# The first three pieces of the float64 weights asked for by ScalarE's queue instead of SP's

## The chip, the cores and the metric

The kernel runs on one core of one Trainium2 chip. The metric is the device time of one execution in microseconds (us); less is better. A core has five engines with a queue each: TensorE (PE in the profile; its weight loads are PEld), VectorE (DVE), ScalarE (ACT), GpSimd (POOL) and SyncE (SP), and 16 DMA engines that all queues feed.

## The reference

An attention block, a mixture of three linear layers joined by a maximum, and a mixture of experts, all on 2304 tokens of 512 numbers:

```
attn  = softmax(mask(scale * q @ k.T)) @ v          # 4 batches, 8 heads, 576 tokens, 64 wide, mask by blocks of 64
x     = attn laid out as (2304, 512)
h     = maximum(maximum(x @ w1, x @ w2), x @ w3)    # w1, w2, w3: (512, 768), given as float64
x     = h @ w_out                                   # (768, 512), float64
score = x @ w_skip;  e = argmax(x @ w_gate)         # 8 experts
out   = x + gate * (max(x @ m2_w1[e], 0) @ m2_w2[e])  where score > 0, else x
```

## The kernel before

The 2304 tokens are taken in six chunks of 384 (three tiles of 128). For each chunk the attention of four pairs of heads is computed in units: one unit is one tile of queries (128 or 64) of one pair of heads in one chunk. A unit goes over PE (scores, `sc`, L611 and a mask matmul L618), DVE (row maximum, L631, scaled at L645), ACT (exponential into `p`, L656), DVE and ACT (reciprocal L671, scaling of `p`, L677 and L679), PE (transposes `tp`, L691), ACT or DVE (copy to `pT`, L696), PE (product with V, `pv`, L710), and ACT and DVE (the result as a high and a low part in `x`, L720 and L718). Scores have two buffers in PSUM (`sc`), so the third unit's scores wait until the first unit's exponentials have read theirs.

The weights w1, w2 and w3 come as float64. Each is cut into six pieces of 128 columns, 18 pieces in all, numbered k = 3f + i for column block f and matrix i. A piece is 512 KB of raw words. It is loaded into `raw` (three buffers, L494), then decoded: ACT takes the absolute value of the upper words (`ab`, L503, into `dec`, two buffers), DVE runs four integer steps (`dec`, L511, L513, L515, L517), ACT rounds to a high part (`hi`, L528), DVE subtracts for the low part (`lo`, L532). A `dec` buffer is free again after `lo`, so the absolute value of piece 2 waits for `lo` of piece 0. Six pieces of w_out follow in the same way. The hidden layer of a chunk (`ps_h`, L736) takes 12 matmuls a piece and can start when all attention of the chunk is in `x`.

The order of all this up to the last chunk is set by a planner: `build` (from L157 on) makes a task of each step with an engine, a duration, a due time, what it depends on and which buffers it takes, and `Plan.order` lays them out engine by engine, taking among the tasks that can start the one with the smallest due time. For a DMA it adds the bytes over one common line of 230 GB/s and 2 us. The tasks are then written out in the order of their planned starts, and each engine runs its own in that order: an instruction that waits holds back all that stand behind it on the same engine. SP's queue holds the loads: K and Q of a group (four transfers of 96 KB, L579 and L580), V (L587), the identity for the transposes (L958) and the raw pieces.

In the kernel before, piece 0 stands in SP's queue behind the loads of the first three groups, pieces 1 and 2 behind those of the fourth.

Of the kernel before, what the change touches and what calls it, by code (L numbers as in the profile page):

```python
# [17 lines left out]
B, H, S, D = 4, 8, 576, 64  # L18
# [138 lines left out]
def build(S, E, groups, units):  # L157
# [4 lines left out]
    def later(name, t, *readers):  # L162
        for r in readers:
            r.releases.append((name, t))
# [18 lines left out]
    for i, (c, b, qlo, qhi, tiles, hp) in enumerate(groups):  # L183
        at = when[first_of[i]] - 12
# [19 lines left out]
    for ks in su:  # L204
        at = when[ks[0]]
        dur, acq, deps = 0.0, [], [start]
        for k in ks:
            i, c, hp, q0, nq, nk, col, first = units[k]
# [5 lines left out]
        for n, k in enumerate(ks):  # L214
            i, c, hp, q0, nq, nk, col, first = units[k]
            at = when[k]
# [37 lines left out]
        for k in ks:  # L254
            i, c, hp, q0, nq, nk, col, first = units[k]
# [10 lines left out]
        for k in ks:  # L266
            i, c, hp, q0, nq, nk, col, first = units[k]
# [19 lines left out]
    later("hm", c1, c2)  # L287
    for k in range(18 + NF):
        at = first_w + w_pace * k if k < 18 else 16 + 3.0 * (k - 18)
        raw = S.add("SP", 0.6, at - 8, lambda k=k: E.raw(k), [], ["raw"], nbytes=524288)  # L290
        ab = S.add("ACT", 0.55, at, lambda k=k: E.ab(k), [raw], ["dec"])
        d = ab
        for n, dur in enumerate((0.335, 0.335, 0.6, 0.6)):
            d = S.add("DVE", dur, at, lambda k=k, n=n: E.dec(k, n), [d])
        later("raw", raw, d)
        hi = S.add("ACT", 0.51, at - 1, lambda k=k: E.hi(k), [d])
        lo = S.add("DVE", 0.6, at - 1, lambda k=k: E.lo(k), [hi])
        later("dec", ab, lo)
        piece[k] = [hi, lo]
        if k >= 18:  # L300
            tw = S.add("PE", 0.45, at, lambda k=k: E.tw(k), [d, c1], ["mo"])
            later("dec", ab, tw)
            wt = S.add("ACT", 0.46, at - 4, lambda k=k: E.wt(k), [tw], ["y"])
            later("mo", tw, wt)
            pw = S.add("PE", 0.9, at, lambda k=k: E.pw(k), [wt], ["mo"])
            wp = S.add("DVE", 0.16, at - 4, lambda k=k: E.wp(k), [pw])
            later("mo", pw, wp)
            later("y", wt, pw)
            piece[k].append(wp)

    prev_y, prev_l, rk_prev = [], [], None
    for c in range(NCH):
# [3 lines left out]
        for f in range(NF):  # L316
            for i in range(3):
                at = base + (3 * f + i) * 2.1
# [22 lines left out]
        at = base + 38  # L341
# [39 lines left out]
    for q in range(8):  # L381
        deps = [go] if q < 3 else [free] if q == 3 else split[q - 4]
        raw = S.add("SP", 0.6, base - 20 + 4 * q, lambda q=q: E.expert_raw(q), deps, nbytes=1 << 20)
        if q < 6:
# [4 lines left out]
            for i in range(2):  # L389
                at = base + 4 * q + 2 * i  # L390
# [54 lines left out]
def _moe1_phase(tc, nc, const, small, g):  # L445
# [12 lines left out]
    with ExitStack() as st_y:  # L458
# [29 lines left out]
        raw_at, dec_at, wt_at, ps_at = {}, {}, {}, {}  # L488

        def raw_words(k):  # L490
            raw = raw_at[k] = apool.tile([P, 4 * P, 2], I32, tag="raw", name="raw", bufs=3)
            if k < 18:
                f, i = divmod(k, 3)
                nc.sync.dma_start(  # L494
                    out=raw.rearrange("p (c f) t -> p c (f t)", c=ND),
                    in_=ws[i][:, 2 * f * P:2 * (f + 1) * P].rearrange("(c p) f -> p c f", p=P))
            else:
                f = k - 18
                nc.sync.dma_start(out=raw.rearrange("p f t -> p (f t)"), in_=w_out[f * P:(f + 1) * P, :])
# [57 lines left out]

        E.wc = wp_copy
        E.raw, E.ab, E.dec, E.hi, E.lo = raw_words, absolute, decode, hi_part, lo_part
        E.tw, E.wt, E.pw, E.wp = wo_turn, wo_turned, wo_route, wo_routed  # L560

# [457 lines left out]

        work = Plan(dict(sc=2, tp=2, mo=2, p=3, pT=2, raw=3, dec=2, hm=4, y=2, k=6, q=3, v=2, x=2))  # L1020
        build(work, E, groups, units)
        with tc.manual_schedule():
            for t in work.order():
# [576 lines left out]
```

## Time and profile before

| | |
|---|---|
| three runs, median (lowest to highest) | 609.37 us (606.86 to 609.39) |
| the profiled execution, its own time | 609.76 us |
| its span, first to last instruction | 607.1 us |
| busy in the span: PE, DVE, ACT | 582.6, 349.8, 316.7 us |
| mean granted TensorE clock | 0.994 |
| first exponential of the attention on ACT | 7.08 us |
| first matmul of the hidden layer (`ps_h`) | 41.33 us |
| first absolute value of a raw piece on ACT | 17.99 us |

The profiled execution lies 0.4 us above the median of the three runs, and its span 2.7 us under its own time. A granted clock of 1.00 is the upper of TensorE's two levels, 2.4 GHz; 0.994 is the mean over the span.

The timeline gives for each instruction its start and length, and in brackets how long its engine had been idle and what ended that. The view by stages gives what each engine was busy in a stretch, so stretch less busy is idle time. SP's row in a timeline is the time that its queue took to issue a transfer; how long that then took to land stands in the list of DMA issues.

### The profile page before, as it was taken

How to read it: one execution, taken by the hardware profiler on the slowest of the kernel's cores; microseconds unless marked ns; L12 is line 12 of the kernel's file. 1: busy time of each engine (PE TensorE's matmuls, PEld its weight loads, DVE VectorE, ACT ScalarE, POOL GpSimd, SP SyncE). 2: the span in 40 equal slices, each digit the busy share in tenths (PEclk: the TensorE clock that was granted, in tenths of full speed). 3: DMA queues.
4: the chain of work that ended last, by engine and by line, in shares of the span. 5: the costliest groups of instructions: out<-in, count | busy, mean ns of one | idle time of the engine just before them, and what ended most of it. 6: DMA issues, size and time to landing. Idle time of an engine off the chain costs nothing. (4 is left out here: it accounts for less than half of the span.)

```text
span 607.1 us, 11847 instructions
## 1 busy us (share of the span) xinstructions
PE 582.6 (96%) x4338; PEld 495.5 (82%) x4338; DVE 349.8 (58%) x1022; ACT 316.7 (52%) x825; POOL 43.3 (7%) x101
## 2 busy tenths in 40 slices
PE   6889999899999999999999999999999999899994
PEld 3568798699888998988978889988899997688732
DVE  4899999925555346555366562565533675258600
ACT  4998869942757424545245444375641541158420
POOL 1000000002000010000200000200001011311101
PEclk9999999999999999999999999999999999899998
DMA  6564754421110220103211223100016752799980
GB/s 184 159 203 140 217 159 142 138 92 60 51 30 23 72 90 24 41 21 94 75 44 48 62 77 110 44 22 23 1 37 213 250 179 49 238 363 366 343 288 23
DMA packets 61096, 72.74 MB, mean 120 GB/s; under 512 B 7571, under 2 KB 40597, under 8 KB 61024
## 3 DMA queue, kind: packets, MB, share of 16 engines
q1 hardware_dynamic: 59424, 68.88, 35.5%
q0 software_dynamic: 1600, 2.96, 1.5%
q8 instruction: 39, 0.64, 0.5%
q14 instruction: 33, 0.27, 0.1%
HBM read 61.13 MB, written 11.04 MB: 119 GB/s over the span
## 5 line engine op out<-in xcount | busy, mean ns | idle before, releaser
L736 PE MATMUL ps_h<-x,w 128*128 128x384 f32 x1296 | 244.7, 341 | 0.5 <-DVE hm L745 0.5
L736 PEld LDWEIGHTS ps_h<-x,w 128*128 128x128 f32 x1296 | 222.4, 188 | 5.5 <-issue 3.3
L656 ACT ACTIVATE p<-sc,nm 128x288 f32<-128x288 f32 (+7 forms) x168 | 85.0, 516 | 29.6 <-DVE nm L645 28.9
L696 ACT COPY pT<-tp 128x512 f32<-128x512 f32 (+2 forms) x108 | 53.3, 511 | 47.9 <-PE tp L691 46.7
L611 PE MATMUL sc<-k,q 64*64 64x288 f32 (+9 forms) x384 | 67.8, 453 | 6.4 <-DMA q<-in_kq_dram 4.7
L691 PE MATMUL tp<-cst_sb,p 128*128 128x128 f32 x432 | 65.9, 281 | 3.9 <-ACT pT L696 1.8
L787 PE MATMUL ps_y<-wo,h_h 128*128 128x256 f32 (+1 forms) x360 | 68.8, 287 | 0.0
L691 PEld LDWEIGHTS tp<-cst_sb,p 128*128 128x128 f32 x432 | 49.7, 143 | 17.7 <-issue 8.0
L710 PE MATMUL pv<-pT,vt 128*64 128x128 f32 (+1 forms) x960 | 60.4, 270 | 1.6 <-ACT pT L696 1.5
L631 DVE TENSOR_REDUCE nm<-sc 128x2 f32<-128x256 f32 (+7 forms) x64 | 51.3, 811 | 15.8 <-PE sc L618 10.3
L710 PEld LDWEIGHTS pv<-pT,vt 128*64 128x64 f32 x960 | 48.0, 138 | 13.8 <-issue 4.9
L787 PEld LDWEIGHTS ps_y<-wo,h_h 128*128 128x128 f32 x360 | 56.7, 189 | 1.2 <-issue 1.2
L787 PE MATMUL ps_y<-wo,h_l 128*128 128x256 f32 (+1 forms) x180 | 51.1, 284 | 0.0
L611 PEld LDWEIGHTS sc<-k,q 64*128 64x128 f32 (+1 forms) x384 | 29.5, 178 | 24.2 <-issue 11.3
L677 ACT ACTIVATE p<-p,r 128x576 f32<-128x576 f32 (+8 forms) x73 | 42.3, 596 | 9.0 <-DVE r L671 8.3
L745 DVE TENSOR_TENSOR hm<-ps_h,ha 128x384 f32<-128x384 f32 x36 | 20.0, 555 | 34.6 <-PE ps_h L736 33.2
L720 ACT CAST x<-pv 128x128 fp32r<-128x128 f32 (+1 forms) x80 | 20.0, 263 | 31.2 <-PE pv L710 30.8
L656 ACT ACTIVATION_READ_ACCUMULATOR p<-sc,nm 128x1 f32 x168 | 35.0, 208 | 0.0
L745 DVE TENSOR_TENSOR hm<-ps_h,hm 128x384 f32<-128x384 f32 x36 | 20.0, 555 | 25.2 <-PE ps_h L736 24.6
L787 PEld LDWEIGHTS ps_y<-wo,h_l 128*128 128x128 f32 x180 | 34.0, 189 | 0.0
L718 DVE TENSOR_TENSOR x<-pv,x 128x128 fp32r<-128x128 f32 (+1 forms) x80 | 21.1, 274 | 21.6 <-ACT x L720 20.8
L749 ACT CAST h_h<-hm 128x384 fp32r<-128x384 f32 x36 | 18.5, 515 | 28.0 <-DVE hm L745 27.9
(220 smaller groups left out, 678.8 us busy)
## 6 DMA issues: line engine op xcount, KB each, us to landing
raw<-in_m_w_dram SPq DMA_DIRECT2D x19, 1024.0 KB, 7.2
raw<-in_w_dram SPq DMA_DIRECT2D x18, 512.0 KB, 3.8
vt<-in_v_dram SPq DMA_DIRECT2D x16, 320.0 KB, 3.3
x<-y SPq DMA_DIRECT2D x18, 256.0 KB, 2.1
out_dram<-y SPq DMA_DIRECT2D x18, 256.0 KB, 2.4
xa<-in_m_w_dram SPq DMA_DIRECT2D x4, 1024.0 KB, 6.8
xb<-in_m_w_dram SPq DMA_DIRECT2D x4, 1024.0 KB, 7.8
raw<-in_w_out_dram SPq DMA_DIRECT2D x6, 512.0 KB, 3.5
```

What stands on the lines that cost most here:

```text
L611: nc.tensor.matmul(bank[:, 0:hi - lo], gd["q"][rows, q0:q0 + nq], gd["k"][rows, lo:hi], start=True, stop=packed or hi != nk)
L631: nc.vector.tensor_reduce(nm, first_ps[:, :, 0:w], axis=AX.X, op=ALU.max, negate=True)
L656: nc.scalar.activation(u["p"][:, j, lo:hi], src, AF.Exp, bias=u["nm"][:, j:j + 1], scale=0.125, accum_out=u["su"][:, n, j:j + 1])
L677: nc.scalar.activation(pt, pt, AF.Copy, scale=r)
L691: nc.tensor.transpose(tp[:, n, :], u["p"][:, j, t * P:(t + 1) * P], ident)
L696: copy(u["pT"][:, m:m + z], u["tp", m][:, 0:z])
L710: nc.tensor.matmul(pv[64 * j:64 * j + 64, 0:nq], vt[:, t, 64 * j:64 * j + 64], pT, start=(t == 0), stop=(t == nkt - 1))
L718: nc.vector.tensor_tensor(xl, pv, xh, op=ALU.subtract)
L720: nc.scalar.copy(xh, pv)
L736: nc.tensor.matmul(ps, a[:, d, :], x[:, d, :], start=(n == 0), stop=(n == 3 * ND - 1))
L745: nc.vector.tensor_tensor(nxt, hm_at["ps", i], hm_at[f], op=ALU.max)
L787: nc.tensor.matmul(ps, a[:, f, hs], x[:, f, lo:hi], start=(n == 0), stop=(n == 3 * NF - 1))
```

## The change

In the planner's `build`, the load of pieces 0, 1 and 2 becomes a task of ACT with the due times -900, -899 and -898 (ahead of all other work but the masks), and it is entered with 150,000 bytes rather than 524,288. In `raw_words` the transfer of these three is issued from ACT's queue. The other 15 pieces and w_out stay with SP. The bytes that move are the same.

```
+        first = k < 3
-        raw = S.add("SP", 0.6, at - 8, lambda k=k: E.raw(k), [], ["raw"], nbytes=524288)
+        raw = S.add("ACT" if first else "SP", 0.6, k - 900 if first else at - 8, lambda k=k: E.raw(k), [], ["raw"],
+                    nbytes=150000 if first else 524288)
...
         def raw_words(k):
+            dma = nc.scalar.dma_start if k < 3 else nc.sync.dma_start
             raw = raw_at[k] = apool.tile([P, 4 * P, 2], I32, tag="raw", name="raw", bufs=3)
             if k < 18:
                 f, i = divmod(k, 3)
-                nc.sync.dma_start(
+                dma(
```

Since the planner lays everything out anew, the order of other work changes too, in the attention of the first chunks. Line numbers of the kernel after are up to 3 higher. On ACT, from the start of the program, before (`warm` is a first exponential that loads the table; `p`, `sc` and `nm` belong to attention units):

```order
L955 ACT_TABLE_LOAD
L955 ACTIVATE warm_135<-warm_135 128x2
L656 ACTIVATE p_186,su_187<-sc_165,nm_181 128x128 x2
L656 ACTIVATE p_191,su_192<-sc_170,nm_184 128x256
L677 ACTIVATE p_186<-p_186,r_199 128x128
```

and on ACT in the same place now:

```order
L497 DMA raw_129<-in_w1_dram 128x4x256
L958 ACT_TABLE_LOAD
L958 ACTIVATE warm_137<-warm_137 128x2
L497 DMA raw_156<-in_w2_dram 128x4x256
L497 DMA raw_158<-in_w3_dram 128x4x256
L506 ACTIVATE dec_163<-raw_129 128x512
L531 CAST w0_113<-dec_163 128x512
L506 ACTIVATE dec_196<-raw_156 128x512
L506 ACTIVATE dec_202<-raw_158 128x512
L659 ACTIVATE p_205,su_206<-sc_177,nm_194 128x128 x2
```

The three issues, the three absolute values and one high part now stand ahead of the first exponential. On DVE, behind the same seven memsets, before:

```order
L631 TENSOR_REDUCE nm_181<-sc_165 128x2
L645 TENSOR_SCALAR nm_181<-nm_181 128x2
L631 TENSOR_REDUCE nm_184<-sc_170 128x2
L645 TENSOR_SCALAR nm_184<-nm_184 128x2
L667 TENSOR_SCALAR r_199<-su_187 128x2
L671 RECIPROCAL r_199<-r_199 128x2
```

and on DVE in the same place now:

```order
L514 TENSOR_SCALAR dec_163<-dec_163 128x512
L516 TENSOR_SCALAR dec_163<-dec_163 128x512
L518 SCALAR_TENSOR_TENSOR dec_163<-raw_129,dec_163 128x512
L520 SCALAR_TENSOR_TENSOR dec_163<-raw_129,dec_163 128x512
L634 TENSOR_REDUCE nm_194<-sc_177 128x2
L535 TENSOR_TENSOR w0_113<-dec_163,w0_113 128x512
L648 TENSOR_SCALAR nm_194<-nm_194 128x2
L634 TENSOR_REDUCE nm_200<-sc_183 128x2
L514 TENSOR_SCALAR dec_196<-dec_196 128x512
L648 TENSOR_SCALAR nm_200<-nm_200 128x2
L516 TENSOR_SCALAR dec_196<-dec_196 128x512
L514 TENSOR_SCALAR dec_202<-dec_202 128x512
```

The decoding of piece 0 (`dec_163`) moved ahead of the first maximum, and steps of pieces 1 and 2 (`dec_196`, `dec_202`) stand among the first units. Up to the first maximum over a hidden layer (L745), DVE had run 29 steps of decoding in the order before and runs 40 in the one after, of them 4 ahead of the first maximum of the attention. On ACT, up to the first copy out of a hidden layer (L741), 11 steps of decoding stood before and 15 stand after, of them 4 ahead of the first exponential.

## Rows read from the trace of the kernel before

**Rows 1.** Busy time by stages: stretch, its length, each engine's busy us (instructions), clock, DMA.

```profile
core 0: us, PE busy (x) PEld busy (x) DVE busy (x) ACT busy (x) POOL busy (x), PEclk, DMA share, GB/s
0.00:20.00 20.00, 13.94 (x88) 8.73 (x88) 10.72 (x45) 11.15 (x37) 1.87 (x13) 1.00 0.71 203
20.00:40.00 20.00, 15.99 (x145) 9.62 (x143) 19.43 (x62) 19.78 (x63) 0.15 (x1) 1.00 0.50 146
...
41.30:122.00 80.70, 78.39 (x643) 66.76 (x640) 77.70 (x212) 67.09 (x174) 2.54 (x13) 1.00 0.55 166
...
120.00:500.00 380.00, 379.37 (x3007) 344.20 (x3006) 195.71 (x601) 182.32 (x502) 22.78 (x53) 1.00 0.22 71
```

**Rows 2.** Timeline of PE: first scores, and first matmuls of the hidden layer.

```profile
4.00 0.76 PE L611 MATMUL sc<-k,q 64*128 64x128 f32 x2 [4.00 <-DMA q<-in_kq_dram]
...
41.33 4.45 PE L736 MATMUL ps_h<-x,w 128*128 128x384 f32 x24
```

**Rows 3.** Timeline of ACT: the table load and the first exponential.

```profile
0.75 1.28 ACT L955 ACT_TABLE_LOAD   x1 [0.75 <-PEq L1587]
...
7.08 0.37 ACT L656 ACTIVATE p<-sc,nm 128x128 f32<-128x128 f32 x1 [4.83 <-DVE nm L645]
```

**Rows 4.** Timeline of DVE: the first maximum and its scaling.

```profile
6.35 0.42 DVE L631 TENSOR_REDUCE nm<-sc 128x2 f32<-128x256 f32 x1 [4.78 <-PE sc L618]
6.81 0.17 DVE L645 TENSOR_SCALAR nm<-nm 128x2 f32<-128x2 f32 x1
```

**Rows 5.** Timeline of SP's queue: first load, and the raw pieces.

```profile
0.74 0.59 SPq L579 DMA_DIRECT2D k<-in_kq_dram  x1
...
9.93 0.59 SPq L494 DMA_DIRECT2D raw<-in_w_dram  x1
...
13.04 1.14 SPq L494 DMA_DIRECT2D raw<-in_w_dram  x2
```

**Rows 6.** DMA issue at 0.74 us: KB, us from issue to landing.

```profile
k<-in_kq_dram SPq DMA_DIRECT2D x1, 96.0 KB, 2.3
```

**Rows 7.** The same for the two issues at 9.93 and 10.56 us.

```profile
raw<-in_w_dram SPq DMA_DIRECT2D x1, 512.0 KB, 4.5
k<-in_kq_dram SPq DMA_DIRECT2D x1, 96.0 KB, 4.3
```

**Rows 8.** Busy time by stages, the first 18 us.

```profile
0.00:4.00 4.00, 0.00 (x1) 0.03 (x1) 0.58 (x7) 1.49 (x2) 1.87 (x13) 1.00 0.37 109
4.00:6.00 2.00, 1.27 (x6) 1.01 (x8) 0.00 (x0) 0.00 (x0) 0.00 (x0) 1.00 0.61 167
6.00:8.00 2.00, 1.43 (x11) 0.77 (x7) 1.19 (x3) 0.81 (x4) 0.00 (x0) 1.00 0.70 195
...
2.00:10.00 8.00, 4.70 (x20) 2.70 (x20) 2.29 (x8) 2.35 (x11) 0.55 (x1) 1.00 0.69 196
...
12.00:14.00 2.00, 2.00 (x10) 1.26 (x10) 1.46 (x7) 1.88 (x7) 0.00 (x0) 1.00 1.02 303
15.00:18.00 3.00, 3.00 (x24) 1.86 (x20) 1.80 (x8) 2.34 (x9) 0.00 (x0) 1.00 1.02 331
```

**Rows 9.** Instructions on the decoded words: duration min/median/max in ns, first and last start.

```profile
L503 ACT ACTIVATE dec<-raw x10: 663/690/708, 18.0 to 56.2; 128x512 f32<-128x512 f32 x10
L511 DVE TENSOR_SCALAR dec<-dec x10: 405/420/427, 18.9 to 58.3; 128x512 f32<-128x512 f32 x10
L513 DVE TENSOR_SCALAR dec<-dec x10: 416/420/428, 19.7 to 58.8; 128x512 int32<-128x512 int32 x10
L515 DVE SCALAR_TENSOR_TENSOR dec<-raw,dec x10: 681/688/693, 20.1 to 59.2; 128x512 int32<-128x512 int32 x10
L517 DVE SCALAR_TENSOR_TENSOR dec<-raw,dec x9: 679/683/691, 21.0 to 57.7; 128x512 int32<-128x512 int32 x9
L528 ACT CAST w<-dec x9: 607/627/659, 22.2 to 58.7; 128x512 fp32r<-128x512 f32 x9
L532 DVE TENSOR_TENSOR w<-dec,w x9: 676/683/692, 24.3 to 59.8; 128x512 fp32r<-128x512 f32 x9
```

## The prediction

> **What bounds the kernel now.** I read the busy times by stages first. From 120 to 500 us PE is busy 379.37 of 380 us [rows 1]: whatever the first 120 us end late or early, the end inherits, since nothing behind can swallow it. So the question is how much time PE loses early. It loses 6.06 us in the first 20 and 4.01 in the next 20 [rows 1], of which 4.00 before its first scores [rows 2] and 0.73 and 0.57 up to 8 us [rows 8]; that leaves 4.77 us between 8 and 40. From 41.3 to 122 us it loses 80.70 - 78.39 = 2.31 us [rows 1]. These 7.1 us are all that a better order could win once the scores have begun.
>
> Then the timelines. The first maximum runs at 6.35, its scaling at 6.81, the first exponential at 7.08 [rows 3, 4]. Up to there ACT and DVE stand idle 4.83 and 4.78 us in one wait: the idle time that is to be filled. From 20 to 40 us both are full (19.78 and 19.43 of 20), and DVE stays so up to 122 us (77.70 of 80.70) [rows 1]. The hidden layer starts at 41.33 [rows 2].
>
> **The change part by part.** *What goes from SP.* Three issues of about 0.59 us [rows 5] leave its queue and later K and Q are asked for sooner. PE's idle time names a DMA only for the first two scores, whose loads stood ahead of the pieces anyway: worth nothing.
>
> *What ACT gets as its first work.* One issue ahead of the table load, two behind it, each 0.59 us by SP's row [rows 5]. Table load and issues end at about 0.75 + 1.28 + 3 x 0.59 = 3.8 us, under the wait that lasts to 7.08 [rows 3]: nothing. Without that cover it would cost 1.8 us.
>
> *What now stands ahead of the first exponential.* In the order after, ACT runs the absolute values of pieces 0, 1 and 2 and the high part of piece 0 before it. The third absolute value needs piece 2 landed, and the buffer that the low part of piece 0 on DVE frees. Behind it wait every exponential; on DVE, a step of piece 2 that stands ahead of the first sums and reciprocals; on PE, the transposes and the third unit's scores, which need a buffer that exponentials free. So the attention starts at the later of two times, plus 0.69 us for that absolute value [rows 9].
>
> First time, the chain over piece 0. A 96 KB load lands 2.3 us after its issue [rows 6]; at 303 GB/s, the rate with several transfers in flight [rows 8], 0.32 us of that is moving, so 2.0 us are fixed. Piece 0 moves 0.524 MB; alone at 331 GB/s [rows 8] that is 1.6 us, landing at 0.75 + 2.0 + 1.6 = 4.35. Absolute value, four steps, high part, low part, third absolute value: 0.69 + 0.42 + 0.42 + 0.69 + 0.68 + 0.63 + 0.68 + 0.69 = 4.90 [rows 9], and eight handovers of 0.07 (from 6.35 to 7.08 pass 0.73 us for 0.42 + 0.17 of work, two handovers [rows 3, 4]) make 0.56: first exponential not before 9.8.
>
> Second time, the landing of piece 2. Three pieces are 1.573 MB. Meanwhile SP goes on asking for K, Q and V: from 2 to 10 us the DMA engines moved 196 GB/s [rows 8] with no piece among it. With several queued they move 303 to 331 [rows 8], 317 in the middle. Which of two queues goes first, no row shows. If the pieces get everything, 1.573 / 0.331 = 4.75 us, landing at 7.5, and the chain above decides: 9.8. If SP is served first, 317 - 196 = 121 are left, 13.0 us, landing at 15.75, exponential at 16.4. With equal shares, 158 each, 9.9 us, landing at 12.65, exponential at 13.3. I take equal shares: with both on SP's queue, K asked for right behind a piece took 4.3 us against 2.3 before and the piece 4.5 [rows 6, 7], so both suffer. Delay against 7.08: **6.3 us**, bounds 2.7 and 9.4.
>
> The Trainium skill's page "DMA: Bandwidth & Descriptors" (section "Queues, rings and completion order") says that each DMA engine goes round robin over the queues that have work, a packet at a time; by that rule the time would be that of equal shares, and no run here shows two hardware queues at once. Its section "Issuing engines are not separate DMA queues" speaks against the change: another issuing engine saves only its issue time.
>
> *What K and Q lose.* Under equal shares their loads move at 158 rather than 196 GB/s, so the first scores at 4.00 come perhaps 1 us later. That is hidden under the 13.3; if the pieces come quickly it is part of the 9.8.
>
> *What is given back.* The decoding done early should lighten the full stretch. By counts of the order it does not do so before the hidden layer starts: ACT has 11 steps of decoding between the first exponential and the first copy out of the hidden layer, before and after (15 less 4); DVE has 29 before and 36 after (40 less 4). The planner has filled the room with later pieces. Seven more steps of some 0.6 us [rows 9], 4 us, go into the idle time of DVE between its first maximum and 18 us. So the hidden layer starts about as much later as the attention, and what is given back comes behind it, where more pieces lie ready: at most the 2.31 us that PE loses there. I take half, **1.1 us**, with bounds 0 and 2.3.
>
> **Sum.** 6.3 - 1.1 = 5.2 us more than the profiled execution's 609.76: 615.0. That execution lies 0.4 above the median of the three runs, 609.37, so for a median: **614.6 us**.
>
> **The rivals.** *Fast landing.* If the pieces take nearly all of the transfers, or SP's loads leave more room than I think, the chain over piece 0 decides: 2.7 us less 0 to 2.3, so 609.8 to 612.1. For it: the DMA share is only 0.61 to 0.70 from 4 to 8 us [rows 8]. Against it: 1.57 MB more in the same time.
>
> *SP first.* If K, Q and V keep their pace, piece 2 lands at 15.75: 9.4 less 0 to 1.1, so 617.7 to 618.8. For it: SP has one short transfer outstanding after the other; against it: nothing known prefers them.
>
> *Faster.* This is what the idle 4.8 us of DVE invite. With the fast landing (+2.7), three pieces would be decoded while the units start: 3 x (0.42 + 0.42 + 0.69 + 0.68 + 0.68) = 8.7 us of DVE's work [rows 9] leave the full stretch, and PE's 4.77 and 2.31 us of losses [rows 1, 8] could all go: 609.4 + 2.7 - 7.1 = 605.0. It decides from where PE's losses between 8 and 40 us shrink by more than the first exponential is late. Against it: the counts, which show no lighter stretch, and that the first exponential must wait for the last of the three pieces.
>
> *The change does not do what it says:* the transfers start at once, but the planner enters 150,000 bytes for 524,288, so its order expects piece 2 sooner than any of the landings above. That is the cause in the forecast, not another case.
>
> **How the numbers follow.** Forecast (equal shares, give or take 2 us) 0.60; fast landing 0.20; SP first 0.11; faster 0.09. A measurement can tell about 0.5%, 3.05 us, from no change: slower means above 612.4, faster below 606.3. The forecast lies above 612.4 but for its edge, SP first wholly, the fast landing within: slower 0.70, same 0.22, faster 0.08. The range goes from the foot of the fast landing, 609.8, to SP first with nothing given back, 618.8; outside lie the faster case and some 0.05 above.
>
> **What would show it.** In the trace after: the first exponential at 13.3 us (9.8 to 16.4), right behind the third absolute value, ACT's idle time before that ended by the raw piece's DMA and not by DVE; the three pieces landing at about 6, 9 and 12.7 us; PE idle some 5 us between the second unit's scores and the first transposes; the hidden layer from about 47 us; PE full behind 120 us as before. Wrong it would be if the third absolute value ran by 10 us, if the hidden layer started before 43 us, or if PE's losses from 41 to 122 us, 2.31 us, were not there to give and more were lost there by the new order.

## The result and the profile after

The changed kernel takes 613.23 us (median; 612.18 to 614.43) against 609.18 for the kernel before on the same chip: 1.0061 times as long, 95% interval 1.0045 to 1.0076. In a second comparison (E6 below) it took 614.72 against 610.36: 1.0083, 1.0061 to 1.0104. By these ratios it is slower by 3.7 and 5.1 us, by the medians by 4.05 and 4.36; the forecast was 5.2 us, 614.6. The execution profiled for the rows below took 613.26 us with a span of 611.2 (before: 609.76 and 607.1).

The timeline of ACT after, from the start (start, length, engine, line, what; in brackets the idle time before it and what ended it):

```profile
0.75 0.43 ACTq L497 DMA_DIRECT2D raw<-in_w_dram  x1
1.21 1.28 ACT L958 ACT_TABLE_LOAD   x1 [1.21 <-PEq L1590]
1.61 1.18 ACTq L497 DMA_DIRECT2D raw<-in_w_dram  x2
...
4.50 0.66 ACT L506 ACTIVATE dec<-raw 128x512 f32<-128x512 f32 x1 [1.79 <-DMA raw<-in_w_dram]
7.56 0.62 ACT L531 CAST w<-dec 128x512 fp32r<-128x512 f32 x1 [2.41 <-DVE dec L520]
9.50 0.66 ACT L506 ACTIVATE dec<-raw 128x512 f32<-128x512 f32 x1 [1.32 <-DMA raw<-in_w_dram]
12.48 0.66 ACT L506 ACTIVATE dec<-raw 128x512 f32<-128x512 f32 x1 [2.32 <-DMA raw<-in_w_dram]
13.05 0.35 ACT L659 ACTIVATE p<-sc,nm 128x128 f32<-128x128 f32 x1
```

The first exponential runs at 13.05, 5.97 us later than in [rows 3], right behind the third absolute value, and that one's idle time was ended by the raw piece's DMA. The three pieces were there at about 4.5, 9.5 and 12.5 us. So far this looks like the forecast (13.3; landings at 6, 9 and 12.7). But PE and DVE show another cause beside it. Their timelines after:

```profile
6.91 0.77 PE L614 MATMUL sc<-k,q 64*128 64x128 f32 x2 [6.91 <-DMA q<-in_kq_dram]
10.35 0.55 PE L614 MATMUL sc<-k,q 64*128 64x128 f32 x1 [2.68 <-DMA q<-in_kq_dram]
...
13.89 1.65 PE L614 MATMUL sc<-k,q 64*128 64x384 f32 x4 [1.65 <-ACT p L659]
...
46.63 3.56 PE L739 MATMUL ps_h<-x,w 128*128 128x384 f32 x19
```

```profile
11.22 0.42 DVE L634 TENSOR_REDUCE nm<-sc 128x2 f32<-128x256 f32 x1 [3.69 <-PE sc L621]
11.56 0.68 DVE L535 TENSOR_TENSOR w<-dec,w 128x512 fp32r<-128x512 f32 x1
12.16 0.16 DVE L648 TENSOR_SCALAR nm<-nm 128x2 f32<-128x2 f32 x1
```

The first scores start at 6.91 instead of 4.00 [rows 2], the next at 10.35, and the first maximum, which waits for them, at 11.22 instead of 6.35 [rows 4]: 4.87 us late before ACT's row has any say. From maximum to exponential passed 0.73 us in before [rows 3, 4]; here pass 1.83. The low part of piece 0 (L535) stands between the maximum and its scaling on DVE and ends at 12.24. The third absolute value needs the buffer that it frees, and starts at 12.48: so it waited for two things that came within a quarter of a microsecond of each other, the landing of piece 2 and a low part that stands behind the late maximum. In E2 below, where the pieces land early, 1.67 us pass from maximum to exponential in the same order. So of the 5.97 us, 4.87 come from late K and Q, about 0.9 from the new order and about 0.2 from the landing of piece 2.

K and Q are late because their transfers land late. From the list of DMA issues, those at 0.74, 1.38, 2.01 and 2.65 us (KB, us from issue to landing):

```profile
k<-in_kq_dram SPq DMA_DIRECT2D x1, 96.0 KB, 4.2
q<-in_kq_dram SPq DMA_DIRECT2D x1, 96.0 KB, 5.4
k<-in_kq_dram SPq DMA_DIRECT2D x1, 96.0 KB, 6.7
q<-in_kq_dram SPq DMA_DIRECT2D x1, 96.0 KB, 7.6
```

In before these four take 2.3 to 2.7 us (the first stands in [rows 6]). The busy times by stages after (stretch, length, busy us of each engine, granted clock, share of the DMA engines, GB/s):

```profile
0.00:20.00 20.00, 7.74 (x36) 4.75 (x38) 10.71 (x38) 9.10 (x27) 1.87 (x13) 1.00 0.68 182
20.00:40.00 20.00, 17.39 (x152) 10.65 (x150) 17.46 (x60) 17.49 (x58) 0.00 (x0) 1.00 0.55 164
120.00:500.00 380.00, 379.19 (x3013) 342.55 (x3013) 198.93 (x614) 178.88 (x502) 23.04 (x54) 1.00 0.23 71
2.00:10.00 8.00, 0.77 (x2) 0.50 (x2) 2.24 (x4) 2.48 (x5) 0.55 (x1) 1.00 1.00 290
```

From 2 to 10 us the DMA engines are now busy all the time (share 1.00 at 290 GB/s; before 0.69 and 196 [rows 8]), and PE works 0.77 us of these 8 instead of 4.70. It loses 12.26 us in the first 20 instead of 6.06 [rows 1], wins 1.4 back in the next 20, and is full from 120 to 500 as before.

The list of DMA queues says whose bytes moved (q1 carries what SP issues, q10 what ACT issues; packets, MB, share of the 16 engines). From 2 to 10 us, before:

```profile
q1 hardware_dynamic: 1721, 1.42, 63.4%
```

and after:

```profile
q10 hardware_dynamic: 1543, 1.54, 65.3%
q1 hardware_dynamic: 781, 0.64, 29.6%
```

ACT's queue moved more than twice as much as SP's, and SP's less than half of what it moved in before, although SP had asked for 736 KB by 6.1 us. At first SP's moved nothing at all: from 2.3 to 3.5 us the list has 398 packets of q10 and none of q1, while the first K load had been asked for at 0.74.

SP's own queue stands still as well. Its waits from 0 to 30 us after (who waited for whom: us in total, times, longest):

```profile
SPq L583 <- DMA raw<-in_w_dram: 5.2, 2, 3.4
```

The built program shows why a Q load waits for a piece of weights: the transfers that SP and ACT issue take eight completion semaphores in turn, and one waits for the transfer that held its semaphore eight earlier. In before these were all SP's own; now three of the eight belong to the 512 KB pieces on ACT's queue, and the second group's loads wait for them (Q at 9.49 instead of 4.93 us). What this costs E4 and E7 tell.

### The profile page after: what moved, and what is told of

It is laid out like the page before. It is cut to its first block, busy times and chain, and to the rows that moved or that the text cites. A ratio compares the mean times of both kernels' runs of the same rounds, so it can differ in the third digit from the quotient of the medians.

```text
span 611.2 us, 11835 instructions
## 1 busy us (share of the span) xinstructions
PE 582.6 (95%) x4338; PEld 494.4 (81%) x4338; DVE 354.2 (58%) x1030; ACT 313.1 (51%) x817; POOL 43.3 (7%) x101
## 5 line engine op out<-in xcount | busy, mean ns | idle before, releaser
L699 ACT COPY pT<-tp 128x512 f32<-128x512 f32 (+2 forms) x102 | 50.0, 508 | 45.7 <-PE tp L694 44.9
L680 ACT ACTIVATE p<-p,r 128x576 f32<-128x576 f32 (+8 forms) x71 | 41.3, 595 | 12.6 <-DVE r L674 12.0
L797 ACT COPY y<-ps_y 128x256 f32<-128x256 f32 x30 | 11.1, 371 | 42.4 <-PE ps_y L790 42.2
```

The costliest lines, as they stand in the source:

```text
L680: nc.scalar.activation(pt, pt, AF.Copy, scale=r)
L699: copy(u["pT"][:, m:m + z], u["tp", m][:, 0:z])
```

## The experiments

All runs in one table; each number is from the timelines and the list of tiles of its profiled execution. "Rest" is the span's end less the start of the last hidden-layer matmul; the ratio is of times to before's on the same chip, with its interval.

| run | first exp | hidden layer | last `ps_h` | rest | time / before |
|---|---|---|---|---|---|
| before | 7.08 | 41.3 | 499.7 | 107.4 | |
| after | 13.05 | 46.6 | 505.8 | 105.4 | 1.0061 (1.0045 to 1.0076) |
| after again, E6 | 12.88 | 46.7 | 506.0 | 106.3 | 1.0083 (1.0061 to 1.0104) |
| old order, early on ACT, E1 | 11.51 | 45.8 | 504.2 | 107.3 | 1.0083 (1.0064 to 1.0102) |
| old order, early on POOL, E7 | 10.94 | 46.0 | 504.4 | 107.3 | 1.0077 (1.0053 to 1.0102) |
| old order, ACT, behind first exp, E4 | 7.25 | 41.8 | 500.2 | 108.3 | 1.0010 (0.9997 to 1.0022) |
| old order, first Q on ACT, E5 | 7.07 | 41.7 | 500.0 | 108.0 | 0.9997 (0.9984 to 1.0011) |
| new order, quarter transfers, E2 | 9.22 | 42.0 | 501.2 | | |
| one piece, its own order, E3 | 9.18 | 41.9 | 503.1 | 107.9 | 1.0071 (1.0049 to 1.0093) |
| one piece again, E8 | 9.05 | 42.3 | 503.5 | 107.5 | |

**E1 to E4** set two theories against each other: the loss comes from the transfers, which hold up K and Q; or from the new order, in which three absolute values stand ahead of the first exponential.

**E1: the transfers alone.** The order of before on all engines, only the three transfers go first on ACT's queue:

```
def raw_words(k, early=False):
    if k < 3 and not early:
        return
    dma = nc.scalar.dma_start if early else nc.sync.dma_start
...
for k in range(3):
    raw_words(k, early=True)
for t in work.order():
```

> The order of the kernel before, word for word, except that the three transfers are issued by ACT as its first work; no decoding stands ahead of the first exponential. Theory B (the block: the third absolute value, which stands ahead of the exponentials on ACT, sets the start of the attention): without it the first exponential comes back to 7 or 8 us, the hidden layer to about 42, the time to 609 to 610. Theory K (the loads: the three transfers alone hold up the first K and Q so long that the attention starts nearly as late): the second half of the first scores waits until about 10.4 as in the kernel after, the first exponential comes 1.6 us behind (as in before: 5.49 to 7.08), at about 12.0, the hidden layer at about 46, the time at 612.5 to 613.5.

Measured 615.23 against 610.21, 1.7 us above the range of theory K. The timeline of PE and ACT:

```profile
7.50 0.77 PE L614 MATMUL sc<-k,q 64*128 64x128 f32 x2 [7.50 <-DMA q<-in_kq_dram]
9.91 0.55 PE L614 MATMUL sc<-k,q 64*128 64x128 f32 x1 [1.65 <-DMA q<-in_kq_dram]
```

```profile
11.51 0.37 ACT L659 ACTIVATE p<-sc,nm 128x128 f32<-128x128 f32 x1 [7.69 <-DVE nm L648]
```

No decoding stands ahead of the exponential, and yet it is 4.43 us late, ended by the scaled maximum on DVE. The hidden layer starts 4.5 late, and its last matmul is 4.5 late. The transfers alone make a loss as large as that of the whole change, and the old order hands the late start on one for one.

**E2: the order alone, as nearly as it goes.** The order of after, but each early transfer brings only the first quarter of its piece; the rest of `raw` is filled with a constant by GpSimd, so these weights are not those of the reference, and the last stage, which depends on the tokens' experts, is not comparable (its one execution took 724.83 us).

```
+                n = 1 if k < 3 else ND
...
-                    out=raw.rearrange("p (c f) t -> p c (f t)", c=ND),
-                    in_=ws[i][:, 2 * f * P:2 * (f + 1) * P].rearrange("(c p) f -> p c f", p=P))
+                    out=raw.rearrange("p (c f) t -> p c (f t)", c=ND)[:, 0:n],
+                    in_=ws[i][:, 2 * f * P:2 * (f + 1) * P].rearrange("(c p) f -> p c f", p=P)[:, 0:n])
```

> The kernel after, with each of the three early transfers cut to a quarter of its bytes (128 KB); the rest of the words is filled by GpSimd. So a part of the weights is wrong, the routing to experts may differ, and only the time up to the last hidden layer is to be read, not the total. Order and semaphores are those of the kernel after. Theory of the prediction (landing sets the start, and the new order alone costs only the chain over piece 0): the pieces land at about 3.5 to 5 us, the first exponential at 8.5 to 9.5, the hidden layer at 42 to 43.5 instead of 46.6. Rival (the new order itself, with 36 steps of decoding instead of 29 on the way, is what makes the hidden layer late): the hidden layer stays at 45 us or later although the first exponential is early.

The timeline of ACT:

```profile
3.17 0.66 ACT L509 ACTIVATE dec<-raw 128x512 f32<-128x512 f32 x1 [0.50 <-DMA raw<-in_w_dram]
6.96 0.62 ACT L534 CAST w<-dec 128x512 fp32r<-128x512 f32 x1 [3.13 <-DVE dec L523]
7.49 0.66 ACT L509 ACTIVATE dec<-raw 128x512 f32<-128x512 f32 x1
8.66 0.66 ACT L509 ACTIVATE dec<-raw 128x512 f32<-128x512 f32 x1 [0.52 <-issue]
9.22 0.36 ACT L662 ACTIVATE p<-sc,nm 128x128 f32<-128x128 f32 x1
```

and of DVE:

```profile
7.55 0.43 DVE L637 TENSOR_REDUCE nm<-sc 128x2 f32<-128x256 f32 x1 [0.62 <-PE sc L624]
7.89 0.68 DVE L538 TENSOR_TENSOR w<-dec,w 128x512 fp32r<-128x512 f32 x1
```

With little to transfer, the chain over piece 0 and the first maximum, which stands ahead of its low part on DVE, give the first exponential at 9.22 (the prediction had it at 9.8), and the hidden layer starts at 42.0, 0.6 late. Of the 2.14 us at the first exponential 1.20 are there at the maximum: the quarter transfers hold up K and Q as well. The last `ps_h` matmul is 1.5 late: from the hidden layer's start to there this order takes 459.2 us, as in after, and before 458.4.

**E3: one early piece** instead of three (`k < 3` becomes `k < 1` in both places), laid out anew by the planner.

> The kernel after with only piece 0 on ACT's queue; pieces 1 and 2 stay with SP and the planner lays out accordingly. Ahead of the first exponential stand on ACT one absolute value and one high part, on DVE the four steps and the low part. Theory K: a third of the early bytes, so the first K and Q are late by about 1.5 us (second half of the scores at about 7.0 instead of 5.49), first exponential at about 8.8 to 9.5 (the low part stands between maximum and scaling), time 610 to 611.5. Theory B (only a wait for piece 2 matters): first exponential at 7.5 to 8, time 608.5 to 609.5.

A miss. The start went as expected (first exponential 9.18, hidden layer 41.9). The second scores come at 6.63 with one piece, at 6.68 with E2's three quarters, at 9.91 and 10.35 with three whole pieces (E1 and after), at 5.49 with none: a third or a quarter of the bytes goes with a delay of 1.1 to 1.2 us, all of them with 4.4 to 4.9. But the time is 613.99 against 610.21. The list of tiles shows the last `ps_h` matmul at 503.1: 2.8 us more are lost between the hidden layer's start and its end, which the first 13 us can't explain. See E8.

**E4: the transfers a little later.** The order of before; the three transfers are issued by ACT behind the first unit's two exponentials:

```
def first_exp(k, j):
    s_exp(k, j)
    if (k, j) == (0, 1):
        for n in range(3):
            raw_words(n, early=True)
```

> The order of the kernel before; the three transfers are issued by ACT behind the exponentials of the first unit (at about 7.5 us, against 9.9 and 13.0 on SP in before). If the loss of the kernel after is all in the first 13 us, before the first exponential, this has none of it: first exponential at 7.1, hidden layer at 41 to 42, time within 1.5 us of before. If early pieces hurt the later loads of K and Q as well (groups 2 to 4), the hidden layer comes 1 to 3 us later and the time is 610.5 to 612. As the decoding stands where it stood, no gain is expected from either.

610.95 against 610.21, ratio 1.0010. The hidden layer starts at 41.8. Here too the transfers hold up loads and SP's queue. SP's waits from 0 to 30 us, and the K load asked for at 8.65 (it belongs to the third group):

```profile
SPq L583 <- DMA raw<-in_w_dram: 6.4, 3, 2.6
k<-in_kq_dram SPq DMA_DIRECT2D x1, 96.0 KB, 8.3
```

Together with ACT's 1.5 us of issues this makes the hidden layer 0.5 us late, and the time longer by no more than the noise. What costs is that the transfers run beside the first loads of K and Q. Nothing is won either.

**E5 to E8** ask what E1 to E4 left open: whether an earlier start is handed on too, whether SP's standing still matters, and what of the traces repeats.

**E5: the other sign.** The order of before; only the first group's two Q loads are issued by ACT as its first work, so that the last of the four first loads is asked for 1.3 us sooner.

```
(nc.scalar if i == 0 else nc.sync).dma_start(out=gd["q"][rows, 0:qhi - qlo], in_=src[:, 2 + j, qlo:qhi])
```

> The order of before, the raw pieces on SP as before; only the first group's two Q loads are issued by ACT, as its first work, while SP issues the two K loads. It asks whether a gain in the first microseconds reaches the end as the losses of the earlier runs did. In before the second Q load is issued at 2.65 and the first maximum follows its scores at 6.35, the first exponential at 7.08. Now the last of the four is asked for at about 1.4 instead of 2.65 us. Theory (the start is inherited one for one in the old order): first scores at about 3.2, first exponential 1.0 to 1.4 us earlier, at 5.7 to 6.1, the hidden layer at 40.0 to 40.4, the time 1.0 to 1.4 below before. Rival (the later K, Q and V loads or the full ACT and DVE between 20 and 40 us set the hidden layer's start): the first exponential comes early, but the hidden layer stays at 41.0 or later and the time is within 0.5 of before.

Neither theory met its case, since the start did not get earlier. The timeline of PE:

```profile
4.02 0.76 PE L614 MATMUL sc<-k,q 64*128 64x128 f32 x2 [4.02 <-DMA k<-in_kq_dram]
5.47 0.55 PE L614 MATMUL sc<-k,q 64*128 64x128 f32 x1 [0.68 <-DMA k<-in_kq_dram]
```

Both times are those of before (4.00 and 5.49). The first K load, asked for at 0.74 as before, lets PE start at 4.02; from 2 to 4 us the DMA engines moved 221 GB/s here and 217 in before. Asked for sooner, the four loads did not land sooner. The DMA engines were not full in this stretch (share 0.85; before 0.74), so what held the loads is not shown. The time is the same, 610.12 against 610.36. Whether an earlier start would be handed on was therefore not tried.

**E6: the changed kernel once more**, unchanged.

> The changed kernel once more, unchanged, for a second trace of its last stage. In its first trace the stretch from the first matmul on psa to the last took 45.7 us against 47.8 in before and 48.1 to 48.3 in three others, PE waited 1.8 us for T there against 2.5, and the granted clock stayed at 1.00 from 520 to 560 where the others show 0.83 to 0.95 in one slice of 10. Theory (this belongs to the changed order): again 45.5 to 46, a wait of 1.6 to 2.0, no slice below 0.98, hidden layer at 46.6 and a time 3 to 5 above before. Rival (chance of that one execution): a stretch of 47.5 or more with a wait near 2.5 and a slice at 0.8 to 0.95.

Half a miss: the first exponential and the hidden layer repeat within 0.2 us (12.88 and 46.7), although the first scores start at 5.58 and not at 6.91. Of the last stage the clock repeats, the wait does not. The busy times by stages in 520 to 540 us, of before:

```profile
520.00:530.00 10.00, 7.51 (x28) 5.67 (x28) 3.78 (x19) 1.18 (x2) 4.79 (x5) 0.83 0.63 176
530.00:540.00 10.00, 9.85 (x48) 7.85 (x47) 4.37 (x6) 3.68 (x5) 1.87 (x2) 1.00 1.01 349
```

of after:

```profile
520.00:530.00 10.00, 8.15 (x43) 6.50 (x42) 2.29 (x10) 0.74 (x2) 0.13 (x1) 1.00 0.69 210
530.00:540.00 10.00, 10.00 (x51) 8.30 (x50) 3.71 (x14) 2.86 (x5) 4.66 (x5) 1.00 0.84 270
```

and of after again:

```profile
520.00:530.00 10.00, 7.80 (x41) 6.24 (x41) 2.39 (x10) 0.74 (x2) 0.00 (x0) 1.00 0.77 212
530.00:540.00 10.00, 8.90 (x45) 7.15 (x44) 3.77 (x15) 2.86 (x5) 4.80 (x5) 1.00 0.81 281
```

In before PE waits 2.48 us for `T` there and the clock is granted at 0.83; 0.17 x 10 = 1.7 us of full speed are lost by that. In both executions of after the clock stays at 1.00. The waits are 1.84 us in the first, 2.18 and another 1.10 in the second. The rest of the span is 2.0 and 1.1 us shorter than in before. E1, E3, E4, E5 and E8 have a clock of 0.83 to 0.89 in one of these two stretches and a rest of 107.3 to 108.3; E7 has 1.00, but waits of 1.8 and 1.5 us, and 107.3. That the clock makes the shorter rest is therefore not shown, nor that it belongs to the order: of the 34 executions of before that stand beside E1 to E8, six have a mean clock of 0.997 over the span, as the first of after has, and their spans (606.1 to 608.8 us) are no shorter than those of the twelve at 0.994 (605.9 to 608.6).

**E7: who issues.** As E1, with GpSimd issuing in ACT's place (`nc.gpsimd.dma_start`); its transfers take no turn in the semaphores of SP's queue.

> The order of before, the three transfers asked for as early as in the run with the old order, but by GpSimd instead of ACT. Then SP's rows no longer take their semaphores in turn with the raw pieces, so SP need not stand still behind them; the bytes in flight are the same. Theory A (the loss comes from sharing the DMA engines in the first 10 us): first loads of K and Q again land 4 us or more after their issue, first scores after 6 us, first exponential at 10 to 12, the time 3 to 5 above before, and SP's queue shows no wait for a raw piece. Theory B (SP's standing still is what costs): first exponential still late by what the first four loads lose, but the loss shrinks behind it and the hidden layer starts at 44 or earlier, the time within 2.5 of before. If GpSimd hands its transfers out slowly, they land late and K and Q are disturbed less: first exponential at 8 to 9, time within 2 of before.

Theory A. SP's queue over the stretch in which it stood still in after:

```profile
4.45 0.50 SPq L582 DMA_DIRECT2D k<-in_kq_dram  x1
4.99 0.60 SPq L583 DMA_DIRECT2D q<-in_kq_dram  x1
5.63 0.59 SPq L582 DMA_DIRECT2D k<-in_kq_dram  x1
6.27 0.59 SPq L583 DMA_DIRECT2D q<-in_kq_dram  x1
```

and PE:

```profile
4.63 0.76 PE L614 MATMUL sc<-k,q 64*128 64x128 f32 x2 [4.63 <-DMA q<-in_kq_dram]
9.35 0.55 PE L614 MATMUL sc<-k,q 64*128 64x128 f32 x1 [3.95 <-DMA q<-in_kq_dram]
```

SP goes on asking up to 6.91, and no wait of its names a raw piece; behind that it stands still too, 3.3 us in all, for loads of its own that land late. The second scores start at 9.35 all the same, the first exponential at 10.94, the hidden layer at 46.0, and the time is 614.05 against 610.36. So it does not matter whether ACT or GpSimd issues. Nor can SP's standing still make the late start: in all these runs the first four loads are asked for from 0.74 to 2.65 us, before any such wait. The bytes in flight make it. (The first scores, expected after 6 us, started at 4.63: GpSimd issues its first piece only at 1.32 us.)

**E8: one early piece once more**, unchanged from E3.

> The run with one early piece once more, for a second trace. In the first, the hidden layer started at 41.9, but the last matmul group of the hidden layer only at 503.1, 2.8 us more than the hidden layer's start was late, with a granted clock of 0.98 from 40 to 122 us. Theory (its new order costs the time): again 502.5 to 503.5 and 0.98. Rival (chance of that execution): 500.5 to 501.5 and 1.00.

The theory: from 42.3 to 503.5 it loses 2.8 us again. The busy times by stages of 100 to 110 us, of before and of E8:

```profile
100.00:110.00 10.00, 8.99 (x98) 7.25 (x97) 8.70 (x34) 8.52 (x29) 0.71 (x4) 1.00 0.55 175
```

```profile
100.00:110.00 10.00, 10.00 (x86) 8.86 (x86) 7.67 (x29) 8.08 (x26) 0.46 (x3) 0.83 0.54 159
```

The granted clock is 0.83 in this stretch in E3 and in E8, which is 1.7 us of the 2.8. This order has the low clock in every execution: the mean over the span is 0.986 to 0.991 in the seven of E3 and E8, and 0.992 to 0.997 in the 34 of before beside E1 to E8. Where the other 1.1 us go, and why the clock falls in this order while PE is full, stays open.

## Why the prediction was right

The time lies 1.4 us under the forecast in the first comparison and 0.1 above it in the second, where the kernel before is 1.0 us slower too; as differences, 4.05 and 4.36 us stand against 5.2. But several steps failed, their errors cancelled in part, and that the number came so close is in part luck. The busy times by stages, up to the hidden layer's start and from there to its last matmul, in which to read what came back, before:

```profile
0.00:41.33 41.33, 31.24 (x236) 18.88 (x236) 31.47 (x109) 31.94 (x101) 2.02 (x14) 1.00 0.59 169
41.33:499.70 458.37, 455.56 (x3624) 409.17 (x3623) 271.38 (x806) 247.64 (x670) 25.13 (x65) 1.00 0.28 88
```

and after:

```profile
0.00:46.63 46.63, 30.59 (x230) 18.41 (x230) 34.79 (x116) 32.02 (x98) 2.05 (x14) 1.00 0.61 172
46.63:505.80 459.17, 457.18 (x3629) 410.19 (x3628) 272.19 (x807) 244.05 (x666) 25.11 (x65) 1.00 0.28 86
```

- **The first exponential**: 6.3 us forecast, 5.97 and 5.80 measured. Piece 2 was forecast to land at 12.65, and the third absolute value found it at 12.48 and 12.31. The time is right, the reason is not. The prediction took equal shares, and set beside them the rule of the Trainium skill's page "DMA: Bandwidth & Descriptors" (section "Queues, rings and completion order"), turns between the queues that have work, a packet at a time. This trace does not show equal shares: ACT's queue moved 1.54 MB from 2 to 10 us, SP's 0.64. At 158 GB/s the pieces would have moved about 1.1 MB by 10 us; they had moved 1.55 of 1.573, and the last 31 packets, 0.03 MB, took until about 12.4. In E1 all of the same three transfers was moved by 10. What held those last packets is not shown.
- **What K and Q lose** is the term that was mis-sized: 1 us forecast, and called hidden; 4.87 measured at the first maximum. It was worked out from a mean rate (158 for 196 GB/s), as if each small load waited in proportion. SP's queue got 80 GB/s from 2 to 10 us (0.64 MB), and nothing from 2.3 to 3.5. [rows 7] held the sign: a K load asked for right behind a single piece took 4.3 us for 2.3. The prediction read it for the shares and not for this price. E1 and E7 make this the cause: with nothing of the decoding ahead of the exponential it is still 4.43 and 3.86 us late.
- **The absolute values ahead of the exponential**, the forecast's cause, are true of the trace but add little: with the low part of piece 0 about 0.9 us by the order, and about 0.2 by the landing of piece 2. The prediction's chain over piece 0 left out that its low part stands behind the first maximum on DVE, so that late K and Q hold up the third absolute value too. If K and Q had been in time, a landing at 12.4 would still have held the exponential; no run shows that case. Two causes of nearly one size lay side by side, and the sum came out right with one of them mis-sized.
- **PE's idle time** lies elsewhere than forecast. Not some 5 us between the second unit's scores and the first transposes: there PE waits 1.65 us, ahead of the third unit's scores. It loses 6.91 and 2.68 us ahead of its first scores, before 4.00 and 0.73.
- **"SP goes on asking for K, Q and V"** failed: its queue stood still for 5.2 us on semaphores that it shares with ACT. The late start is not its doing, since the first four loads had been asked for before. What it costs behind that is not separated; in E4 6.4 us of it, with the late loads, go with 0.5 us at the hidden layer.
- **What is given back** was forecast at 1.1 (0 to 2.3) behind the hidden layer's start, from PE's idle time. Behind the start PE is idle 1.99 us instead of 2.81: 0.8 come back where the forecast had them. But PE is busy there 1.6 us longer, of which 0.65 are matmuls that stood ahead of the start in before (236 there, now 230); where the rest comes from is not shown. So nothing is left of the gain at the last `ps_h` matmul, which is 6.1 us late. What did come back, 2.0 and 1.1 us, came in the last stage. The prediction's "nothing behind can swallow it" holds up to 500 us and not behind it.
- **The rivals.** Fast landing would have needed the third absolute value by 10 us; only E2's quarter transfers did that. SP first would have shown the first scores near 4.00 us; they came at 6.91. Its ground, one short transfer outstanding after the other, does not fit before's own rows: the first four loads were asked for within 1.9 us and took 2.3 to 2.7 each. Faster fell with the start. The prediction's own test, hidden layer from about 47 us, PE full behind 120, met 46.63 and 379.19 of 380.
- **The rule against the change**, of the Trainium skill's page "DMA: Bandwidth & Descriptors" (section "Issuing engines are not separate DMA queues"; another issuer saves only issue time), agrees with E4 and E5: 1.0010 and 0.9997.

In the old order the delay of the hidden layer's start passes to its end within 0.1 us (E1 4.5 to 4.5, E4 0.5 to 0.5, E5 0.4 to 0.3, E7 4.7 to 4.7). No version tried beats the kernel before.

## What to carry to other kernels

A transfer that is not needed yet, put ahead of small loads that the first work waits for, is not free because its own queue is idle: the DMA engines were busy with it all the time from 2 to 10 us, and here 1.5 MB asked for some 6 us sooner than in E4 cost 4 to 5 us, whether ACT or GpSimd asked. Price such a move by what the first consumer's loads lose when the DMA share goes to 1.00, not by a mean rate; and put it behind those loads (E4), where no cost clear of the noise was left. When a change shifts everything behind it, look at each stage for itself, the last one too.

## What the runs showed of the hardware

- Three 512 KB pieces in flight made 96 KB loads on another queue land 4.2 to 7.6 us after issue instead of 2.3, while the first piece itself, asked for at 0.75, was there at 4.5. The two queues did not share equally: 1.54 MB of ACT's and 0.64 of SP's from 2 to 10 us, and 398 packets to none from 2.3 to 3.5.
- Asking sooner did not help by itself: in E5 the last of four loads was asked for 1.3 us sooner, and the scores that wait for them started at 4.02 and 5.47 instead of 4.00 and 5.49.
- A transfer on ACT's queue can stop SP's queue through completion semaphores taken in turn: 5.2 us of waits in after, 3.5 in E1, 6.4 in E4, none on a raw piece in E7.
- The granted clock can fall while PE is full: in both profiled executions of E3's order it is 0.83 from 100 to 110 us, where PE is busy 10.00 of 10 us and was busy 9.97 and 9.94 of the 10 us before. In before it is 0.83 from 520 to 530 us, where PE waits 2.48 us.
